# A leaky activation in place of a sign pass, and another order of work, in a fused attention and feed-forward kernel

## The chip, the core and the metric

The kernel runs on one core of one Trainium2 chip. The metric is device time in microseconds (us), from the first to the last instruction with what the runtime puts around them. The core has five engines with queues of their own: TensorE (PE; its weight loads are shown apart as PEld), VectorE (DVE), ScalarE (ACT), GpSimd (POOL) and SyncE (SP), which here only starts DMAs. Each engine works through its queue strictly in order, and waits on semaphores for the others. PE writes to PSUM, and POOL reads and writes SBUF alone.

## The reference

Two parts, one behind the other. The first is a linear attention over 4 batches x 4 heads x 1088 tokens of 32 numbers, in float32; the second a feed-forward layer of width 2048 on the 4352 tokens of 128 numbers that come out. The weights `w_in` and `w_out` come as float64.

```python
def phi(x):                                   # 8 x 8 products per token and head
    a = np.einsum('rd,bhsd->bhsr', S1, x)
    b = np.einsum('rd,bhsd->bhsr', S2, x)
    return np.einsum('bhsi,bhsj->bhsij', a, b).reshape(*x.shape[:-1], r * r)
q_p, k_p = phi(q), phi(k)
kv  = np.einsum('bhsf,bhsd->bhfd', k_p, v)
z   = np.sum(k_p, axis=2)
num = np.einsum('bhsf,bhfd->bhsd', q_p, kv)
den = np.einsum('bhsf,bhf->bhs', q_p, z)[..., None] + 1e-06
x   = (num / den)                             # -> (4352, 128)

h     = x @ w_in
g     = h * np.clip(h + 3.0, 0.0, 6.0) / 6.0
out   = (g @ w_out).astype(np.float32)
```

## The kernel before, in words

*Tokens.* They are cut into nine chunks: 0 to 7 of 512 tokens, 8 of 256. Keys and values come in nine tiles of 128 tokens per batch, loaded as two groups of 4 and 5 tiles (`k0`, `k1` and `v0`, `v1` are batch 0).

*Attention.* For the keys, `mm_kN` multiplies by S1 and S2 on PE, `cp_kN` copies the result to SBUF on ACT, `outer_kN_t` forms the 8 x 8 products (tile `kph`, on POOL or DVE), and `kvt_b_i` adds up keys times values on PE, in PSUM. Chunk 0 is done the long way: `outer_q0` (tile `qph`), transposes `tr`, copies `trcp`, then `nd` (numerators and denominators, tile written by L499), `norm` on DVE (L504 to L507), the transposes `xt` back (L511), and x split into a high and a low part, `xhi` and `xlo`. Between the key sums and `nd` of batch 0 lie `twice` (ACT copies the sums), `fold` and `zmm` (PE), `spread` (DVE) and `halves` (ACT). Chunks 1 to 8 take a shorter way through `proj`, `cp`, `prod`, `invert`, `divide`, `outer`, `turn`, `move` (eight DMAs) and `xmm`.

*Feed-forward.* For each chunk c and each of eight pairs fp of 128-wide blocks of the 2048, one step: `h` and `l` are six matmuls on PE into a PSUM bank (high x by high and low weights, low x by high weights, L627 to L631), `relu` on ACT (L638), `gate` on DVE (L641), `ghi` on ACT (the high part of g, tile `gh`, L644), `glo` on POOL or DVE (the low part, tile `gl`, L647), then `o` (four matmuls) and `p` (two) by w_out on PE (L664). The first two steps of chunk 0 in the order do `h` in halves of 256 tokens. `h` has two PSUM banks, so the `h` of a step waits for the `gate` of two steps before.

*Weights.* They arrive as raw float64 words, in blocks `wi0` to `wi4` of w_in (256, 256, 512, 512 and 512 columns) and `wo0` to `wo3` of w_out (512 each), and are rebuilt as float32 on the chip: `scale` (ACT, L337) takes the upper 32 bits as a float and multiplies by 2^-112, `sign` (DVE, L343) keeps the sign bit in a PSUM bank, `shift` (DVE, L347) shifts the scaled word left by 3 and puts the sign back, `rest` (ACT, L340) scales the lower 32 bits, `word` (POOL, L351) adds the two, `high` (ACT, L354) and `low` (POOL or DVE, L357) split the result in two parts. The same is done once for S1 and S2, at the start (L291 to L296).

*Loads.* SP starts them one by one (L322); with 128 partitions they have, in KB: S 80, `kN` 256 or 320, `vN` 264 or 330, `qN` 256, weight blocks 256 or 512.

*Order.* `ORDER` is a written list of 1089 steps. `Plan.run` goes through it and emits each step on its engine (`:V` after a name picks DVE where a step may go to two engines, letters in lower case pick a PSUM tag) and hands out buffers in that order. The list alone thus sets each queue. `warm` is a matmul on ones whose result is not used.

Of the kernel before, what the change touches and what calls it, by code (L numbers as in the profile page):

```python
# [14 lines left out]
F32 = mybir.dt.float32  # L15
F32R = mybir.dt.float32r
U32 = mybir.dt.uint32
# [5 lines left out]
P = 128  # L23
# [34 lines left out]
SIGN = 0x80000000  # L58
# [44 lines left out]
s_copy low_wi1 scale_wi2 low_wi0 fold_0 zmm trcp_0_0 scale_wo1 halves tr_0_2:o shift_wi2 nd_0_0 sign_wo1:o shift_wo1 word_wi2 trcp_0_2 rest_wo1
high_wi2 keep_0 ld_q1 ld_k3 ld_k2 ld_wi3 ld_v2 ld_k5 ld_v3 nd_0_2:h norm_0_0 ld_wi4 norm_0_2 xt_0_0:h proj_1:a:o xt_0_2 low_wi2:V cp_1_0 cp_1_1
word_wo1 high_wo1 low_wo1 prod_1 xhi_0_0 xhi_0_1 mm_k2 mm_k3 ld_wo0 ld_q3 ld_q2 cp_k2 cp_k3 scale_wi3 xlo_0_0 xlo_0_1 h_0_3_1 l_0_3_1 rest_wi3
outer_k2_0:V sign_wi3:o invert_1 outer_k2_2:V shift_wi3 h_0_0_1_0 h_0_3_0 l_0_3_0 relu_0_3 l_0_0_1_0 h_0_0_0_0 h_0_0_1_1 kvt_1_0:o l_0_0_0_0 h_0_0_0_1
l_0_0_1_1 l_0_0_0_1 kvt_1_1 relu_0_0 outer_k3_2:V gate_0_3 outer_k3_0 outer_k3_4 divide_1 outer_1_1 mm_k5 kvt_1_2 kvt_1_3 kvt_1_4 kvt_1_5 kvt_1_6
kvt_1_7 kvt_1_8 h_0_2_0 h_0_2_1 l_0_2_0 l_0_2_1 word_wi3 outer_1_0 cp_k5 high_wi3 ghi_0_3 twice_1 scale_wi4 ld_k4 gate_0_0 turn_1_1 h_0_1_0_0
l_0_1_0_0 h_0_1_0_1 l_0_1_0_1 fold_1 h_0_1_1_0 turn_1_0 sign_wi4:o relu_0_2 low_wi3 rest_wi4 scale_wo0 keep_1 glo_0_3 l_0_1_1_0 h_0_1_1_1 l_0_1_1_1
o_0_3 outer_k5_4:V shift_wi4 word_wi4 move_1 ld_wo2 ld_q4 ld_v4 p_0_3 ld_v5 ld_wo3 ghi_0_0 gate_0_2 sign_wo0:h shift_wo0 proj_23:o:a ld_k6 ld_q5  # L110
h_0_5_1 h_0_5_0 l_0_5_1 l_0_5_0 relu_0_1 glo_0_0 ghi_0_2 o_0_2 rest_wo0 high_wi4 relu_0_5 outer_k5_0:V cp_2_0 gate_0_1 h_0_4_1 l_0_4_1 h_0_4_0 l_0_4_0
cp_2_1 outer_k5_2:V cp_3_1 cp_3_0 word_wo0 mm_k4 xmm_1:a:o high_wo0 low_wi4 relu_0_4 prod_3 low_wo0 gate_0_5 xhi_1_1 xhi_1_0 h_0_6_0 h_0_6_1 l_0_6_0
l_0_6_1 gate_0_4 h_1_1_0 h_1_1_1 ghi_0_1 o_0_1 relu_0_6 glo_0_2:V xlo_1_0 xlo_1_1 cp_k4 l_1_1_1 l_1_1_0 relu_1_1 ghi_0_4 glo_0_1 invert_3 gate_0_6
p_0_2 outer_k4_0:V o_0_0 h_1_2_0 h_1_2_1 l_1_2_1 l_1_2_0 p_0_0 divide_3 prod_2 outer_3_0 gate_1_1 h_0_7_0 h_0_7_1 invert_2 p_0_1 l_0_7_0 l_0_7_1
glo_0_4:V scale_wo2 relu_1_2 ghi_1_1 relu_0_7 outer_k4_2:V kvt_2_0 kvt_2_1 kvt_2_2 kvt_2_3 kvt_2_4 kvt_2_5 kvt_2_6 kvt_2_7 kvt_2_8 divide_2 outer_3_1
outer_2_0 glo_1_1 gate_1_2 h_1_3_0 h_1_3_1 l_1_3_1 l_1_3_0 rest_wo2 twice_2 o_1_1 fold_2 out_0_3 ghi_1_2 glo_1_2 turn_3_0 turn_3_1 gate_0_7 h_1_0_1
h_1_0_0 l_1_0_0 l_1_0_1 p_1_1 sign_wo2 o_1_2 shift_wo2 sign_wo3:o keep_2 scale_wo3 relu_1_3 relu_1_0 rest_wo3 turn_2_0 shift_wo3 ld_q7 p_1_2
proj_45:a:o gate_1_3 h_1_5_0 ghi_1_3 ghi_0_5 gate_1_0 h_1_7_0 l_1_7_0 h_1_7_1 h_1_5_1 l_1_5_0 ghi_1_0 l_1_5_1 o_1_3 outer_2_1 word_wo2 word_wo3
# [24 lines left out]
o_5_4 p_5_1 p_4_7 xlo_6_0 glo_5_4 relu_5_5 xlo_6_1 h_6_0_1 l_6_0_1 h_6_0_0 l_6_0_0 glo_5_2:V glo_4_6 o_4_6 p_4_4 relu_6_0 ghi_5_0 glo_5_0 gate_5_5
h_6_4_0 o_5_7 p_5_2 o_5_2 l_6_4_0 h_6_4_1 l_6_4_1 relu_6_4 gate_6_0 ghi_6_0 h_5_3_0 l_5_3_0 h_5_3_1 l_5_3_1 o_5_0 p_4_6 ghi_5_5 glo_5_7 xlo_7_1 p_5_7
gate_6_4 h_6_2_0 h_6_2_1 l_6_2_1 l_6_2_0 p_5_0 o_5_5 glo_5_5:V relu_5_3 gate_5_3 h_6_1_0 h_6_1_1 l_6_1_1 l_6_1_0 relu_6_2 ghi_6_4 out_4_7 glo_6_4
# [88 lines left out]
def fused_kernel(ctx: ExitStack, tc: tile.TileContext, inputs, places, outT):  # L234
# [18 lines left out]
    def at(buf):  # L253
        return room[buf.tag][buf.slot]
# [73 lines left out]
    def weights(nm, hi, lo, j):  # L328
# [24 lines left out]
        def high(_):  # L353
            nc.scalar.copy(hi, at(wb)[:, :n])  # L354
# [406 lines left out]
```

## Time and profile before

| | |
|---|---|
| three runs, median | 228.77 us (228.6 to 228.99) |
| the profiled execution | 227.95 us, of which its span is 226.2 us |
| PE busy | 219.7 us, 97% of the span |
| DVE, ACT, POOL busy | 163.1, 165.9 and 153.7 us |
| HBM read and written | 11.30 MB and 2.23 MB |

The span runs from the first to the last instruction; all times below count from its start. "Idle before" of an instruction is how long its engine had done nothing, with what it waited for behind an arrow. The lengths of PE's matmuls overlap: one is shown with its latency, so the pace is the distance from one start to the next.

### The profile page before, as it was taken

To read this page: it belongs to the slowest core of one execution; us is meant where nothing else is said; L and a number is where in the kernel's file an instruction comes from. 1 tells how busy PE (TensorE), PEld (TensorE's weight loads), DVE (VectorE), ACT (ScalarE), POOL (GpSimd) and SP (SyncE) were. 2 spreads that over 40 slices of the span, in tenths; PEclk is the share of its full clock that TensorE was granted. 3 is DMA by queue.
4 is the path that set the end of the run, shared out by engine and by line. 5 is a ranking of instruction groups with operands and counts; after the bars stand their busy time and mean duration, and the time that the engine had idled before them with its cause. 6 is when DMAs were issued, how large, how long until landed. Compare 5 with 4: busy or idle time off the path is not lost.

```text
span 226.2 us, 4762 instructions
## 1 busy us (share of the span) xinstructions
PE 219.7 (97%) x1888; PEld 174.9 (77%) x1888; DVE 163.1 (72%) x216; ACT 165.9 (73%) x231; POOL 153.7 (68%) x111
## 2 busy tenths in 40 slices
PE   8789999999999999999999999999999999999994
PEld 3568768877788788777887888788888788888993
DVE  2799999999949889677866865686378644648561
ACT  4687997989785878656687865876686777785781
POOL 3859998998199734993899797356640498564471
PEclk9999999999999999999999999999999999999999
DMA  6997149233600001233001113020010000020010
GB/s 206 395 412 281 48 118 380 82 83 78 193 3 0 3 0 47 50 81 130 0 1 48 49 46 93 25 71 0 0 46 3 0 0 0 3 93 0 0 51 23
DMA packets 9430, 17.77 MB, mean 79 GB/s; under 512 B 1728, under 2 KB 2368, under 8 KB 9408
## 3 DMA queue, kind: packets, MB, share of 16 engines
q1 hardware_dynamic: 9408, 17.46, 23.2%
q8 instruction: 15, 0.25, 0.5%
q14 instruction: 7, 0.06, 0.1%
HBM read 11.30 MB, written 2.23 MB: 60 GB/s over the span
## 4 chain that ended last, share of the span: by engine, by line
PE 87%; DVE 5%; POOL 3%; DMA 1%; ACT 1%; issue 0%; SPq 0%; DVEq 0%
PE o L664 41%; PE h L627 14%; PE h L631 13%; PE h L628 13%; PE a L547 2%; DMA raw<-weights_dram 1%; DVE kph L385 1%; PE o L405 1%; PE a L542 1%; POOL gl L647 1%; DVE o L343 1%; POOL w L351 1%; DVE w L347 1%; PE a L375 1%; POOL wi_lo L357 1%; POOL kph L385 0%
## 5 line engine op out<-in xcount | busy, mean ns | idle before, releaser
L647 POOL TENSOR_TENSOR gl<-g,gh 128x1024 fp32r<-128x1024 f32 (+1 forms) x45 | 106.3, 2372 | 56.7 <-ACT gh L644 38.4
L641 DVE SCALAR_TENSOR_TENSOR g<-g,h 128x1024 f32<-128x1024 f32 (+1 forms) x72 | 82.8, 1153 | 35.4 <-ACT g L638 35.2
L638 ACT ACTIVATE g<-h 128x1024 f32<-128x1024 f32 (+1 forms) x72 | 70.7, 982 | 35.3 <-PE h L631 20.7
L644 ACT CAST gh<-g 128x1024 fp32r<-128x1024 f32 (+1 forms) x72 | 70.2, 1002 | 11.0 <-DVE g L641 6.0
L627 PE MATMUL h<-xh,wi_hi 128*128 128x512 f32 (+1 forms) x148 | 56.2, 381 | 0.0
L628 PE MATMUL h<-xh,wi_lo 128*128 128x512 f32 (+1 forms) x148 | 55.1, 373 | 0.0
L664 PE MATMUL o<-gh,wo_hi 128*128 128x512 f32 (+1 forms) x144 | 54.2, 379 | 0.0
L664 PE MATMUL o<-gh,wo_lo 128*128 128x512 f32 (+1 forms) x144 | 54.0, 378 | 0.0
L631 PE MATMUL h<-xh,wi_hi 128*128 128x512 f32 (+1 forms) x148 | 49.9, 374 | 0.0
L664 PE MATMUL o<-gl,wo_hi 128*128 128x512 f32 (+1 forms) x144 | 41.3, 380 | 0.1
L647 DVE TENSOR_TENSOR gl<-g,gh 128x1024 fp32r<-128x1024 f32 (+1 forms) x27 | 33.1, 1235 | 5.9 <-PE o L664 3.6
L627 PEld LDWEIGHTS h<-xh,wi_hi 128*128 128x128 f32 x148 | 27.8, 188 | 7.5 <-DVE g L641 1.2
L631 PEld LDWEIGHTS h<-xh,wi_hi 128*128 128x128 f32 x148 | 27.7, 188 | 5.5 <-DVE xh L470 0.2
L628 PEld LDWEIGHTS h<-xh,wi_lo 128*128 128x128 f32 x148 | 27.8, 188 | 4.6
L664 PEld LDWEIGHTS o<-gh,wo_hi 128*128 128x128 f32 x144 | 27.1, 188 | 5.3 <-issue 0.4
L664 PEld LDWEIGHTS o<-gh,wo_lo 128*128 128x128 f32 x144 | 27.1, 188 | 4.9
L664 PEld LDWEIGHTS o<-gl,wo_hi 128*128 128x128 f32 x144 | 26.0, 188 | 5.5 <-POOL gl L647 0.5
L590 POOL TENSOR_TENSOR qph<-ab 128x512 f32<-128x512 f32 (+1 forms) x16 | 16.1, 1018 | 0.2
L351 POOL TENSOR_TENSOR w<-w,r 128x512 int32<-128x512 int32 (+1 forms) x9 | 10.4, 1166 | 2.5 <-DVE w L347 2.0
L597 DVE STREAM_TRANSPOSE raw<-qph 128x512 f32<-128x512 f32 (+1 forms) x16 | 10.4, 665 | 1.9 <-POOL qph L590 1.9
L385 DVE TENSOR_TENSOR kph<-a,ab 128x512 f32<-128x512 f32 (+1 forms) x14 | 8.8, 635 | 0.5 <-ACT ab L378 0.5
L405 PE MATMUL o<-kph,v 128*32 128x64 f32 x288 | 6.2, 223 | 1.1 <-DVE kph L385 1.0
(104 smaller groups left out, 160.1 us busy)
## 6 DMA issues: line engine op xcount, KB each, us to landing
raw<-weights_dram SPq DMA_DIRECT2D x7, 512.0 KB, 6.3
phT<-raw SPq DMA_DIRECT2D x56, 64.0 KB, 2.0
qT<-tokens_dram SPq DMA_DIRECT2D x8, 256.0 KB, 6.0
outT_dram<-os SPq DMA_DIRECT2D x8, 256.0 KB, 2.2
v<-tokens_dram SPq DMA_DIRECT2D x4, 330.0 KB, 4.8
kT<-tokens_dram SPq DMA_DIRECT2D x4, 320.0 KB, 5.7
v<-tokens_dram SPq DMA_DIRECT2D x4, 264.0 KB, 6.1
kT<-tokens_dram SPq DMA_DIRECT2D x4, 256.0 KB, 5.7
```

Source lines behind the costliest of these rows:

```text
L351: nc.gpsimd.tensor_tensor(w, w, at(rb)[:, :n], op=ALU.add)
L385: engines[e].tensor_tensor(out, a_, b_, op=ALU.mult)
L590: engines[e].tensor_tensor(out, a_, b_, op=ALU.mult)
L597: nc.vector.transpose(turned_view()[:, :, r * half : (r + 1) * half].rearrange("p f (t w) -> p t f w", w=Q), src)
L627: nc.tensor.matmul(at(hb)[:, u, i:k], wi_hi[:, f], x, start=True, stop=False)
L628: nc.tensor.matmul(at(hb)[:, u, i:k], wi_lo[:, f], x, start=False, stop=False)
L631: nc.tensor.matmul(at(hb)[:, u, i:k], wi_hi[:, f], at(x_buf[c])[:, 1, i:k], start=False, stop=True)
L638: nc.scalar.activation(at(gb)[:, :, :n], at(hb)[:, :, :n], AF.Relu, bias=3.0, scale=1.0)
L641: nc.vector.scalar_tensor_tensor(at(gb)[:, :, :n], at(gb)[:, :, :n], 6.0, at(hb)[:, :, :n], op0=ALU.min, op1=ALU.mult)
L644: nc.scalar.copy(at(gh)[:, :, :n], at(gb)[:, :, :n])
L647: engines[e].tensor_tensor(at(gl)[:, :, :n], at(gb)[:, :, :n], at(gh)[:, :, :n].bitcast(F32), op=ALU.subtract)
L664: nc.tensor.matmul(at(ob)[:, :n], w, x[:, :n], start=left == acc["all"] and i == 0, stop=left == 1 and i == len(pairs) - 1)
```

## The change

1. `scale` becomes a leaky activation (`Prelu`) with the slope -2^32 for negative inputs. A negative word comes out positive with its exponent raised by 32, and the shift by 3 moves that bit to the sign's place. So `sign` is gone, and `shift` is a shift with one input, in place. The same holds for S1 and S2.
2. `rest`, `word`, `high`, `cp_k`, `trcp`, `xhi` and `ghi` may run on one of two engines, as the order says.
3. `far_queries` may take chunks of different sizes together; the groups of chunks stay (1), (2, 3), (4, 5), (6, 7), (8).
4. `ORDER` is another list, found by a search in which loads came as late as recorded and all durations were varied at random. It has 8 `warm` in place of 11. 19 `ghi`, 7 `xhi`, 2 `rest`, a `cp_k`, a `word` and a `high` now go to DVE, and of `glo` 33 in place of 27, of `low` 3 in place of 2.

```diff
-SIGN = 0x80000000
+SIGN = -(2.0**32)
 ORDER = """
-ld_k0 warm warm warm warm warm warm warm s_rep s_tr mm_k0:h ld_wi0 scale_wi0 warm warm warm s_back ld_k1 mm_k1 sign_wi0:o shift_wi0 rest_wi0 cp_k0 outer_k0_2 ld_wi1 sign_wi1 outer_k0_0:V
+s_copy warm warm warm warm warm warm s_rep ld_k0 ld_k1 warm mm_k0:a cp_k0 outer_k0_0 outer_k0_2:V mm_k1:a cp_k1 outer_k1_2 outer_k1_0:V ld_q0 mm_q0:h
...
+    def copy(e, out, src):
+        (nc.scalar.copy if e == ACT else engines[e].tensor_copy)(out, src)
...
         def scale(_):
-            nc.scalar.activation(at(wb)[:, :n], words(at(raw)[:, :n])[0].bitcast(F32), AF.Copy, bias=0.0, scale=REBIAS)
+            nc.scalar.activation(at(wb)[:, :n], words(at(raw)[:, :n])[0].bitcast(F32), AF.Prelu, bias=0.0, scale=REBIAS, alpha=SIGN)
...
-        def sign(_):
-            nc.vector.tensor_scalar(bank(sb_)[:, :n].bitcast(U32), words(at(raw)[:, :n])[0], SIGN, None, op0=ALU.bitwise_and)
+        def rest(e):
+            low = words(at(raw)[:, :n])[1]
+            if e == ACT:
+                nc.scalar.activation(at(rb)[:, :n], low, AF.Copy, bias=0.0, scale=2.0**-29)
+            else:
+                nc.vector.tensor_scalar(at(rb)[:, :n], low, 2.0**-29, None, op0=ALU.mult)
         def shift(_):
             w = at(wb)[:, :n].bitcast(U32)
-            nc.vector.scalar_tensor_tensor(w, w, 3, bank(sb_)[:, :n].bitcast(U32), op0=ALU.logical_shift_left, op1=ALU.bitwise_or)
+            nc.vector.tensor_scalar(w, w, 3, None, op0=ALU.logical_shift_left)
...
-        b = plan.add(f"rest_{name}", ACT, [ld], rest, [raw, rb])
-        o = plan.add(f"sign_{name}", DVE, [ld], sign, [raw, sb_])
-        o = plan.add(f"shift_{name}", DVE, [a, o], shift, [wb, sb_])
-        o = plan.add(f"word_{name}", POOL, [o, b], word, [wb, rb])
-        o = plan.add(f"high_{name}", ACT, [o], high, [wb])
+        b = plan.add(f"rest_{name}", (ACT, DVE), [ld], rest, [raw, rb])
+        o = plan.add(f"shift_{name}", DVE, [a], shift, [wb])
+        o = plan.add(f"word_{name}", (POOL, DVE), [o, b], word, [wb, rb])
+        o = plan.add(f"high_{name}", (ACT, DVE), [o], high, [wb])
...
-            a = plan.add(f"xhi_{c}_{k}", ACT, after, xhi, [xps, xh])
+            a = plan.add(f"xhi_{c}_{k}", (ACT, DVE), after, xhi, [xps, xh])
...
-        high = plan.add(f"ghi_{c}_{fp}", ACT, [o], ghi, [gb, gh])
+        high = plan.add(f"ghi_{c}_{fp}", (ACT, DVE), [o], ghi, [gb, gh])
```

The loads on SP, from the start of the program, before (`raw` is a weight block: here `wi0`, `wi1`, `wi2`, `wo1`; `kT` holds keys, `qT` queries, `v` values):

```order
L288 DMA sb_raw<-weights_dram 128x80
L322 DMA kT_78<-tokens_dram 128x512
L322 DMA raw_74<-weights_dram 128x256
L322 DMA kT_79<-tokens_dram 128x640
L322 DMA raw_75<-weights_dram 128x256
L322 DMA qT_81<-tokens_dram 128x512
L322 DMA v_127<-tokens_dram 128x528
L322 DMA v_128<-tokens_dram 128x660
L322 DMA raw_76<-weights_dram 128x512
L322 DMA raw_77<-weights_dram 128x512
L322 DMA qT_82<-tokens_dram 128x512
L322 DMA kT_80<-tokens_dram 128x640
```

and now (`raw` is `wi1`, `wi0`, `wi2`, `wo1`):

```order
L291 DMA sb_raw<-weights_dram 128x80
L324 DMA kT_78<-tokens_dram 128x512
L324 DMA kT_79<-tokens_dram 128x640
L324 DMA qT_81<-tokens_dram 128x512
L324 DMA v_127<-tokens_dram 128x528
L324 DMA raw_74<-weights_dram 128x256
L324 DMA v_128<-tokens_dram 128x660
L324 DMA raw_75<-weights_dram 128x256
L324 DMA raw_76<-weights_dram 128x512
L324 DMA qT_82<-tokens_dram 128x512
L324 DMA raw_77<-weights_dram 128x512
L324 DMA kT_80<-tokens_dram 128x512
L324 DMA kT_78<-tokens_dram 128x640
```

Keys, queries and values of batch 0 move ahead of the first blocks of w_in, and `wi0` goes from third to eighth place.

DVE's queue from S's words on, before (`w` is a weight block, `o` and `a` PSUM banks with sign bits, `kph` and `qph` outer products):

```order
L294 SCALAR_TENSOR_TENSOR s_word<-s_word,s_sign 128x80
L343 TENSOR_SCALAR o_70<-raw_74 128x256
L347 SCALAR_TENSOR_TENSOR w_119<-w_119,o_70 128x256
L343 TENSOR_SCALAR a_72<-raw_75 128x256
L385 TENSOR_TENSOR kph_88<-h_68,ab_84 128x512
L347 SCALAR_TENSOR_TENSOR w_120<-w_120,a_72 128x256
L385 TENSOR_TENSOR kph_89<-a_73,ab_85 128x512 x2
L385 TENSOR_TENSOR qph_90<-h_69,ab_86 128x512 x2
L343 TENSOR_SCALAR o_71<-raw_76 128x512
L427 TENSOR_TENSOR z_diag<-mask,o_70 128x256
```

and now (L346 is `rest`, L360 `low`):

```order
L296 TENSOR_SCALAR s_word<-s_word 128x80
L387 TENSOR_TENSOR kph_88<-a_72,ab_84 128x512
L387 TENSOR_TENSOR kph_89<-a_73,ab_85 128x512
L387 TENSOR_TENSOR qph_90<-h_68,ab_86 128x512
L350 TENSOR_SCALAR w_119<-w_119 128x256
L387 TENSOR_TENSOR qph_90<-h_68,ab_86 128x512
L346 TENSOR_SCALAR r_122<-raw_75 128x256
L350 TENSOR_SCALAR w_120<-w_120 128x256
L360 TENSOR_TENSOR wi_lo<-w_119,wi_hi 128x256
L429 TENSOR_TENSOR z_diag<-mask,o_70 128x256
```

The outer products come first, and of the three of keys that DVE had one goes to POOL; the sign passes are gone, and `spread` (`z_diag`) comes as the tenth row in both.

PE's queue around the first feed-forward matmul, before (`h1` takes chunk 0's x back from the transpose by `ident`, `s_all` is S, `kT` the keys of batch 1):

```order
L511 MATMUL h1_69<-ident_132,x0_94 128x128 x2
L542 MATMUL a1_73<-qT1_82,s_proj_146 32x256 x4
L542 MATMUL o1_71<-qT1_82,s_proj_146 32x256 x4
L511 MATMUL h1_69<-ident_132,x0_94 128x128 x2
L375 MATMUL a0_72<-s_all_162,kT0_78 32x2x32 x16
L375 MATMUL a1_73<-s_all_162,kT2_80 32x2x32 x20
L627 MATMUL h0_68<-xh0_95,wi_hi_64 128x512
```

and now:

```order
L546 MATMUL a0_72<-qT1_82,s_proj_146 32x256 x4
L546 MATMUL o0_70<-qT1_82,s_proj_146 32x256 x4
L513 MATMUL h1_69<-ident_132,x0_94 128x128 x2
L377 MATMUL a1_73<-s_all_160,kT2_80 32x2x32 x16
L513 MATMUL h1_69<-ident_132,x0_94 128x128 x2
L377 MATMUL a0_72<-s_all_160,kT0_78 32x2x32 x20
L632 MATMUL h0_68<-xh0_95,wi_hi_64 128x256
```

The first group of batch 1's keys now stands between the two transposes, and the first feed-forward step works on half of the chunk.

## Rows read from the trace of the kernel before

**Rows 1.** The page: busy time, and slices of PE and its granted clock.

```profile
PE 219.7 (97%) x1888; PEld 174.9 (77%) x1888; DVE 163.1 (72%) x216; ACT 165.9 (73%) x231; POOL 153.7 (68%) x111
...
PE   8789999999999999999999999999999999999994
...
PEclk9999999999999999999999999999999999999999
```

**Rows 2.** The chain that ended last, in order of time: start, length, what.

```profile
78.91 2.27 PE o L664 x10
...
218.60 4.33 PE o L664 x36
```

**Rows 3.** Timeline of PE: start, length, instruction [idle before <- releaser].

```profile
9.92 0.32 PE L405 MATMUL o<-kph,v 128*32 128x64 f32 x8 [1.04 <-DVE kph L385]
...
10.75 0.66 PE L489 MATMUL a<-ident,qph 128*128 128x128 f32 x4
...
13.22 0.69 PE L499 MATMUL a<-kvb,phT 128*64 128x66 f32 x16
...
15.89 0.44 PE L511 MATMUL h<-ident,x 128*128 128x128 f32 x2
16.26 1.21 PE L375 MATMUL a<-s_all,kT 128*32 128x64 f32 x72
17.41 0.50 PE L627 MATMUL h<-xh,wi_hi 128*128 128x512 f32 x1
...
26.77 0.40 PE L664 MATMUL o<-gh,wo_lo 128*128 128x512 f32 x1
27.25 0.73 PE L664 MATMUL o<-gl,wo_hi 128*128 128x512 f32 x2
```

**Rows 4.** Timeline of DVE: S's words, signs and shifts, the norms.

```profile
2.64 0.20 DVE L293 TENSOR_SCALAR s_sign<-sb_raw 128x80 uint32<-128x80 uint32 x1 [0.93 <-DMA sb_raw<-weights_dram]
2.95 0.24 DVE L294 SCALAR_TENSOR_TENSOR s_word<-s_word,s_sign 128x80 uint32<-128x80 uint32 x1
...
6.74 0.43 DVE L343 TENSOR_SCALAR a<-raw 128x256 uint32<-128x256 uint32 x1 [1.03 <-DMA raw<-weights_dram]
...
13.41 0.69 DVE L347 SCALAR_TENSOR_TENSOR w<-w,o 128x512 uint32<-128x512 uint32 x1
14.02 0.16 DVE L504 TENSOR_SCALAR den<-a 128x8 f32<-128x8 f32 x1
...
14.79 0.16 DVE L504 TENSOR_SCALAR den<-h 128x8 f32<-128x8 f32 x1
```

**Rows 5.** Timeline of ACT: passes that waited for a weight block.

```profile
4.75 0.45 ACT L337 ACTIVATE w<-raw 128x256 f32<-128x256 f32 x1 [1.68 <-DMA raw<-weights_dram]
...
10.19 0.70 ACT L340 ACTIVATE r<-raw 128x512 int32<-128x512 uint32 x1 [0.58 <-DMA raw<-weights_dram]
```

**Rows 6.** Windows: stretch, PE, PEld, DVE, ACT, POOL busy, clock, DMA, GB/s.

```profile
40.00:50.00 10.00, 10.00 (x136) 7.95 (x135) 9.93 (x15) 8.63 (x16) 9.46 (x8) 1.00 0.23 65
60.00:80.00 20.00, 20.00 (x176) 15.96 (x154) 14.99 (x20) 14.96 (x19) 15.51 (x11) 1.00 0.07 25
```

**Rows 7.** Timeline of DVE: two subtractions of a low part.

```profile
56.48 1.86 DVE L647 TENSOR_TENSOR gl<-g,gh 128x1024 fp32r<-128x1024 f32 x1
...
147.60 1.22 DVE L647 TENSOR_TENSOR gl<-g,gh 128x1024 fp32r<-128x1024 f32 x1
```

**Rows 8.** Timeline of POOL: instructions beside those of rows 7 and rows 4.

```profile
12.66 1.28 POOL L351 TENSOR_TENSOR w<-w,r 128x512 int32<-128x512 int32 x1 [1.62 <-DVE w L347]
...
55.97 1.30 POOL L357 TENSOR_TENSOR wo_lo<-w,wo_hi 128x512 fp32r<-128x512 f32 x1
...
148.26 2.83 POOL L647 TENSOR_TENSOR gl<-g,gh 128x1024 fp32r<-128x1024 f32 x1 [5.05 <-PE o L664]
```

**Rows 9.** The key loads started in the first 30 us.

```profile
DMA to landing us min/median/max: 2.6/6.7/8.4
```

**Rows 10.** Groups of DVE by line and shape: busy us, mean ns.

```profile
L647 DVE TENSOR_TENSOR gl<-g,gh 128x1024 fp32r<-128x1024 f32 x24 | 30.9, 1294 | 4.8 <-PE o L664 2.5 <-ACT gh L644 1.9 <-ACT ab L378 0.4
```

More of the change, by code (lines that the diff above doesn't have):

```diff
@@ L103 @@
[L103 to L106, printed above, removed]
@@ L333, in weights, with word, high @@
         ld, raw = load("raw", name, lambda t: t[:, :n])
-        wb, rb, sb_ = Buf(("w",)), Buf(("r",)), Buf(ANY)
+        wb, rb = Buf(("w",)), Buf(("r",))
         def scale(_):
-            nc.scalar.activation(at(wb)[:, :n], words(at(raw)[:, :n])[0].bitcast(F32), AF.Copy, bias=0.0, scale=REBIAS)
-        def rest(_):
-            nc.scalar.activation(at(rb)[:, :n], words(at(raw)[:, :n])[1], AF.Copy, bias=0.0, scale=2.0**-29)
-        def sign(_):
-            nc.vector.tensor_scalar(bank(sb_)[:, :n].bitcast(U32), words(at(raw)[:, :n])[0], SIGN, None, op0=ALU.bitwise_and)
+            nc.scalar.activation(at(wb)[:, :n], words(at(raw)[:, :n])[0].bitcast(F32), AF.Prelu, bias=0.0, scale=REBIAS, alpha=SIGN)
[5 more added lines that the diff above has]
+                nc.vector.tensor_scalar(at(rb)[:, :n], low, 2.0**-29, None, op0=ALU.mult)
         def shift(_):
             w = at(wb)[:, :n].bitcast(U32)
-            nc.vector.scalar_tensor_tensor(w, w, 3, bank(sb_)[:, :n].bitcast(U32), op0=ALU.logical_shift_left, op1=ALU.bitwise_or)
-        def word(_):
+            nc.vector.tensor_scalar(w, w, 3, None, op0=ALU.logical_shift_left)
+        def word(e):
             w = at(wb)[:, :n].bitcast(I32)
-            nc.gpsimd.tensor_tensor(w, w, at(rb)[:, :n], op=ALU.add)
-        def high(_):
-            nc.scalar.copy(hi, at(wb)[:, :n])
+            engines[e].tensor_tensor(w, w, at(rb)[:, :n], op=ALU.add)
+        def high(e):
+            copy(e, hi, at(wb)[:, :n])
         def low(e):
@@ L387, in features @@
         o1 = plan.add(f"mm_{name}", PE, [ld], mm, [src, pb, ab])
-        o2 = plan.add(f"cp_{name}", ACT, [o1], cp, [pb, ab])
+        o2 = plan.add(f"cp_{name}", (ACT, DVE), [o1], cp, [pb, ab])
         parts = []
@@ L513, in queries @@
             a = plan.add(f"tr_{c}_{t}", PE, [parts[t], parts[t + m - 1]], tr, [ph, pb, phT])
-            a = plan.add(f"trcp_{c}_{t}", ACT, [a], trcp, [pb, phT])
+            a = plan.add(f"trcp_{c}_{t}", (ACT, DVE), [a], trcp, [pb, phT])
             a = plan.add(f"nd_{c}_{t}", PE, [a, kv_done["near"]], nd, [phT, nb, x])
@@ L520, in far_queries @@
     def far_queries(cs):
-        n = CHUNKS[cs[0]][1]
-        half, blocks = n // 2, n // 2 // Q
+        sizes = [CHUNKS[c][1] for c in cs]
+        offs = [sum(sizes[:k]) // 2 for k in range(len(cs))]
         pbs, xpbs = ([Buf(("a", "o")) for _ in range(2)] for _ in range(2))
@@ L526, in far_queries @@
         for k, c in enumerate(cs):
-            c0 = CHUNKS[c][0]
+            c0, n = CHUNKS[c]
+            half = n // 2
             cuts = [i for i in range(n) if i in (0, half) or batch_of(c0 + i) != batch_of(c0 + i - 1)] + [n]
             spans += [(k, i // half, batch_of(c0 + i), i, j) for i, j in zip(cuts, cuts[1:])]
-            lq, qb = load("qT", f"q{c}", lambda t: t[:, :n])
+            lq, qb = load("qT", f"q{c}", lambda t, n=n: t[:, :n])
             loads.append(lq)
@@ L536, in part @@
         def part(banked, k, r, i, j):
-            return bank(banked[r])[:, k * half + i - r * half : k * half + j - r * half]
+            i0 = offs[k] - r * sizes[k] // 2
+            return bank(banked[r])[:, i0 + i : i0 + j]
         def proj(_):
@@ L550, in far_queries @@
         for k, c in enumerate(cs):
-            moves.append(quotient(c, n, projected_by, [(pbs[r], k * half) for r in range(2)], moved[k]))
+            moves.append(quotient(c, sizes[k], projected_by, [(pbs[r], offs[k]) for r in range(2)], moved[k]))
         xhs = [Buf(("xh",)) for _ in cs]
@@ L554, in far_queries @@
         for k, c in enumerate(cs):
-            split(c, [(k * half, r * half, (r + 1) * half, [o], xpbs[r]) for r in range(2)], xhs[k])
+            half = sizes[k] // 2
+            split(c, [(offs[k], r * half, (r + 1) * half, [o], xpbs[r]) for r in range(2)], xhs[k])
     def quotient(c, n, o, sources, phT):
@@ L641, in gate, with ghi @@
             nc.vector.scalar_tensor_tensor(at(gb)[:, :, :n], at(gb)[:, :, :n], 6.0, at(hb)[:, :, :n], op0=ALU.min, op1=ALU.mult)
-        def ghi(_):
-            nc.scalar.copy(at(gh)[:, :, :n], at(gb)[:, :, :n])
+        def ghi(e):
+            copy(e, at(gh)[:, :, :n], at(gb)[:, :, :n])
         def glo(e):
```

133 lines of the change are left out of this document (68 added, 65 removed).

## The prediction

> **What bounds the kernel now.** Read the page's busy line and slices first [rows 1]: PE is busy 97% of the span, at 7 or 8 tenths in the first three slices of 40 and 9 in every later one but the last, and the granted clock reads 9 throughout. The chain that ended last says the same [rows 2]: stretches of PE alone, ten 512-column matmuls in 2.27 us (0.227 each) at 79 us, and 36 of 256 columns in 4.33 us (0.120 each) up to 222.93. So a matmul in the middle is neither late nor slow. Only less work on PE, or an earlier start of the pile, can shorten the run, and the work is the same in both kernels. The feed-forward part has 756 matmuls of 512 columns (8 chunks x 8 pairs x 12, less the 12 that chunk 0 does in halves) and 120 of 256 (those 24 halves, and chunk 8's 96): 171.6 + 14.4 = 186.0 us. Its first one starts at 17.41 [rows 3], and from there to 222.93 are 205.5 us; the 19.5 left over are attention work of the later batches and chunks, with a small loss at each switch between the two kinds. PE's timeline shows one clear wait behind 17.41: a matmul starts at 26.77, the next could at 27.00, and it starts at 27.25 [rows 3].
>
> What is left to look at is the 17.41 us in front. There PE waits for others, 1.04 us for key features from DVE at 9.92 [rows 3], then for copies, norms and transposes that follow each other. DVE is the engine that is full early on: 9.93 of 10 us from 40 to 50, against 14.99 of 20 from 60 to 80 [rows 6].
>
> **The change, part by part.**
>
> *Sign pass gone.* Ten DVE instructions vanish: 0.20 us on the S words, 0.43 for each of the two 256-wide blocks, and for each of seven 512-wide ones 0.69 (I take the shift's row of that width): 5.9 us. Four of the blocks' passes (2.2 us) stand ahead of the first norm [rows 4].
>
> *The shift alone.* It had two inputs, one in PSUM, and took 0.69 at 512 wide [rows 4]. Now it has one and stays in SBUF. The nearest rows are the two on the S words, both 80 wide and SBUF to SBUF: 0.20 with one input, 0.24 with two [rows 4]. From 256 to 512 wide a pass grows by 0.26 (0.43 to 0.69), 0.0010 per element, so 0.04 is 40 of the 80 elements: the one-input form runs at half the time per element, 0.42 at 512 wide. Bounds 0.42 and 0.69; I take 0.42, since that row has the form itself. DVE saves another 2 us by it.
>
> *Leaky activation for a scaled copy.* No row shows one. Bounds: the copy's time (0.45 at 256 wide, 0.70 at 512 [rows 5]) or twice that. I take the copy's, the same instruction with another function. Twice would put 0.45 + 0.70 + 0.70 more on ACT ahead of the second norm, some 1.4 us with the waits it has there, and that is the whole gain below.
>
> *Work that may go to DVE.* 19 of 72 `gh` copies, 7 of 18 x copies, two `rest` passes, six more `gl` subtractions (33 for 27) and a few of the weights' last steps go there. A subtraction with two SBUF inputs takes 1.22 [rows 7]; a copy as wide lies between that and, at half the time per element, 0.68. With 0.68 the copies are 13 us, the subtractions 7, the rest some 5, and DVE goes from 163 to about 180 of 226. The first `gh` copy that moves is in chunk 1, past 60 us, where DVE has 5 of 20 us free [rows 6]; that room hides them. Without it each would hold the next gate, and PE, which eats a pair in 2.7 us (12 x 0.227).
>
> *Loads in another order.* SP starts them in turn, and the bytes come at one rate: block 0 of w_in is there at 4.75, block 2 at 10.19 [rows 5], with 1938 KB from the one to the other, 356 KB per us. By that rate the new order brings k0 at 4.0, k1 at 4.9, q0 at 5.7, v1 at 8.0 (8.8 before) and block 0 of w_in at 8.75.
>
> *The path to the first matmul.* Before: the last five key tiles' sums run from 9.92 to 10.75, the numerators start at 13.22, the two norms at 14.02 and 14.79, the last transpose at 15.89, batch 1's keys take 16.26 to 17.41 [rows 3, 4]. After:
> - Key sums: the outer products stand first on DVE, with no weight pass between, so v1 decides: start 8.1, and with the same 0.83 the end is at 8.95.
> - ACT copies the sums. Ahead of that copy stand two weight passes, the first of which waits for w_in's block 0: 8.75 + 0.45 + 0.45 = 9.65. Before, the copy could start as the sums ended, at 10.75. This point is 1.1 us earlier.
> - From there to the numerators it took 13.22 - 10.75 = 2.47. ACT now has a 256-wide cast (I take 0.45) where a 512-wide pass (0.70) was: 2.2. Numerators at 11.9.
> - First norm 0.8 later (14.02 - 13.22), at 12.7. The second came 0.77 behind it; a 512-wide shift (0.42) now stands between: 13.9.
> - Last transpose 1.10 later (15.89 - 14.79), at 15.0, and 0.37 long (to 16.26). Of batch 1's keys 16 of 36 matmuls now stand ahead of it; the other 20 take 20/36 of 1.15, 0.64. First matmul at 16.0.
>
> That is 1.4 us earlier. Behind it, up to some 43 us, DVE loses three sign passes and gains on three shifts (3 x 0.96 = 2.9), and takes over an x copy and a subtraction (0.4 + 1.2): 1.3 less, about what PE starts earlier. So PE should wait no more than before; I count neither the 0.25 at 27.25 as won nor a new wait as lost.
>
> **A rule weighed.** A DVE subtraction with two SBUF inputs that starts at 56.48, with POOL in an instruction until 57.27, takes 1.86 in place of 1.22 [rows 7, 8]; a POOL one that starts at 148.26, with DVE in such a subtraction until 148.82, takes 2.83 [rows 7, 8]. They wait for each other's end. The old shift did not: at 13.41 it takes its 0.69 beside a POOL add that runs until 13.94 [rows 4, 8]. The Trainium skill ("SBUF — State Buffer", section "SBUF: two separate sides") says that DVE and GpSimd share a port pair which one of them holds for a whole instruction, and that DVE takes it with two SBUF inputs and in a two-port performance mode too. The rows agree on the first; none shows the second. If it holds, the new shifts and copies join the subtractions in waiting for POOL, and that is the last rival below, priced from rows.
>
> **Sum.** The profiled execution took 227.95 around its span of 226.2; 227.95 - 1.4 = 226.55. The runs' median is 228.77, 0.8 above; 228.77 - 1.4 = 227.4. What differs by under 0.2% (0.46 us) can't be told from no change.
>
> **Rivals.**
> - *More.* ACT's copy of the sums comes right behind them at 9.2 (w_in's block 0 early by as much), and the 0.25 goes too: 1.4 + 0.45 + 0.25 = 2.1, 226.7; with the shift between the norms hidden as well (0.42), 226.2. For it: fewer DVE passes everywhere. Against: block 0 stands behind v1 in the queue. Chance 0.17.
> - *Nothing.* Batch 1's keys now stand on PE around the last transpose, so their load is in front of everything. By the rate k3 (3874 KB in) is there at 14.0, against a need at 15.4; of the key loads before one took 8.4 us from issue to landing [rows 9]. If it lands at 16.8, or the leaky activation takes twice the copy, the gain is gone: 228.8. Chance 0.13.
> - *Slower.* The ports: three shifts and two or three subtractions on DVE lie between the first matmul and 43 us, where POOL has hardly a pause (9.46 of 10 us from 40 on [rows 6]). At 0.64 each (1.86 - 1.22) they add 3.2 to 3.8 us to DVE, against the 1.3 it has less to do and the 1.4 won: 0.5 to 1.1 slower, 229.6. It decides from 2.7 us of such waits on. For it: the rows on waits, and DVE full to 9.93 of 10. Against: the 24 full subtractions of this trace take 1.294 on average [rows 10], so most met no wait. Chance 0.13.
>
> **Chances.** Forecast (0.9 to 1.9 less) 0.57, *more* 0.17, *nothing* 0.13, *slower* 0.13. So faster 0.74, within 0.2% 0.13, slower 0.13. The range takes in all of *nothing*, most of *more* and the nearer part of *slower*, 226.0 to 229.0.
>
> **What will show it.** The first feed-forward matmul between 15.5 and 16.5, the last key sums from about 8.1, the numerators at 11.9; shifts of 0.42 and leaky activations of 0.70 at 512 wide; from the first matmul to the end of PE 205.5 or a little less. Wrong would be: a first matmul at 17 or later; PE idle behind DVE's gates between 20 and 45; shifts of 1 us and more that end as a POOL instruction ends; a slice of the granted clock below 9.

## The result, and the profile after

The changed kernel takes 226.12 us (median of 4 runs, 225.89 to 226.47), the kernel before 228.82 beside it (228.6 to 228.99): a ratio of 0.9883, 95% interval 0.9867 to 0.9899, or 2.7 us. The forecast was 227.4, 1.4 us less than before. The sign was right, the size half of what came.

The page of the changed kernel: busy time of PE and DVE, two rows of the 40 slices, the chain's shares.

```profile
PE 218.4 (97%) x1885; PEld 175.5 (78%) x1885; DVE 182.2 (81%) x244; ACT 147.7 (66%) x201; POOL 144.2 (64%) x103
...
PE   8889999999999999999999999999999999999994
...
PEclk9999999999999999999999999999999999999998
...
PE 93%; DMA 2%; SPq 1%; ACT 1%; issue 1%
```

PE is the bound as before, with an 8 where [rows 1] has a 7; DVE went from 163 to 182 us, as forecast (about 180). The timeline of PE ahead of the first feed-forward matmul (start, duration, work, idle time in brackets) answers to [rows 3]:

```profile
8.74 0.32 PE L407 MATMUL o<-kph,v 128*32 128x64 f32 x8 [0.67 <-DMA v<-tokens_dram]
...
12.06 0.69 PE L501 MATMUL o<-kvb,phT 128*64 128x66 f32 x16 [0.56 <-ACT kvb L438]
...
13.88 0.33 PE L513 MATMUL h<-ident,x 128*128 128x128 f32 x1
14.71 0.27 PE L513 MATMUL h<-ident,x 128*128 128x128 f32 x1 [0.50 <-issue]
14.91 0.65 PE L377 MATMUL a<-s_all,kT 128*32 128x64 f32 x32
15.49 0.44 PE L513 MATMUL h<-ident,x 128*128 128x128 f32 x2
15.86 0.77 PE L377 MATMUL a<-s_all,kT 128*32 128x64 f32 x40
16.56 0.39 PE L632 MATMUL h<-xh,wi_hi 128*128 128x256 f32 x1
```

The last five key tiles start when v1 is there (8.74 for 9.92), the numerators at 12.06 for 13.22, the first feed-forward matmul at 16.56 for 17.41. ACT's and DVE's timelines, against [rows 4] and [rows 5]: copy of the sums, leaky activation of 512 columns, norm, shift of 512, norm.

```profile
9.96 0.26 ACT L441 COPY kvt<-o 128x128 f32<-128x128 f32 x1
...
10.72 0.68 ACT L339 ACTIVATE w<-raw 128x512 f32<-128x512 f32 x1
```

```profile
12.80 0.17 DVE L506 TENSOR_SCALAR den<-o 128x8 f32<-128x8 f32 x1 [0.60 <-PE o L501]
...
13.57 0.42 DVE L350 TENSOR_SCALAR w<-w 128x512 uint32<-128x512 uint32 x1
13.91 0.16 DVE L506 TENSOR_SCALAR den<-h 128x8 f32<-128x8 f32 x1
```

Two more traces, one of each kernel, were taken later. Side by side, worked out from the starts of all matmuls (a matmul's share is the time to the next start; "lost at switches" is what the row ahead of work of another kind and the row behind it take beyond 0.227 or 0.120, the first feed-forward matmul among them):

| us | before | before again | after | after again |
|---|---|---|---|---|
| profiled execution | 227.95 | 229.31 | 226.31 | 226.14 |
| last part of k1 lands | 5.52 | 7.51 | 4.86 | 4.91 |
| first feed-forward matmul | 17.41 | 18.80 | 16.56 | 16.78 |
| from there to PE's end | 205.51 | 205.48 | 204.62 | 204.36 |
| of it: switches, lost at them | 17, 3.28 | 17, 3.27 | 11, 2.23 | 11, 2.22 |
| of it: other losses of feed-forward rows | 0.75 | 0.53 | 0.45 | 0.45 |
| of it: attention work, its waits within | 15.31 | 15.50 | 15.77 | 15.51 |

The rest, 186.17 us in each, is the feed-forward work that the prediction counted as 186.0. So about 1.0 us (0.86 to 1.15) came behind the first feed-forward matmul, where none was forecast, by these rows mostly from six switches fewer. And the trace that the sum started from was of an execution whose loads came early: of 73 runs of before, in five comparisons, one was below its 227.95.

### The profile page after: what moved, and what is told of

Same layout as the page of the kernel before. It is cut to its first block, busy times and chain, and to the rows that moved or that the text cites. A ratio compares the mean times of both kernels' runs of the same rounds, so it can differ in the third digit from the quotient of the medians.

```text
span 224.4 us, 4722 instructions
## 1 busy us (share of the span) xinstructions
PE 218.4 (97%) x1885; PEld 175.5 (78%) x1885; DVE 182.2 (81%) x244; ACT 147.7 (66%) x201; POOL 144.2 (64%) x103
## 3 DMA queue, kind: packets, MB, share of 16 engines
HBM read 11.30 MB, written 2.23 MB: 60 GB/s over the span
## 4 chain that ended last, share of the span: by engine, by line
PE 93%; DMA 2%; SPq 1%; ACT 1%; issue 1%
PE o L669 42%; PE h L632 14%; PE h L633 14%; PE h L636 14%; DMA raw<-weights_dram 2%; PE o L407 2%; PE a L377 2%; PE a L546 1%; PE a L551 1%; SPq L324 1%; PE o L551 1%; ACT w L339 1%; PE o L546 0%; PE h L513 0%; PE o L501 0%
## 5 line engine op out<-in xcount | busy, mean ns | idle before, releaser
L652 POOL TENSOR_TENSOR gl<-g,gh 128x1024 fp32r<-128x1024 f32 (+1 forms) x39 | 92.1, 2364 | 60.9 <-ACT gh L254 34.2
L254 ACT CAST gh<-g 128x1024 fp32r<-128x1024 f32 (+1 forms) x53 | 53.2, 1011 | 19.3 <-PE o L669 16.7
L632 PE MATMUL h<-xh,wi_hi 128*128 128x512 f32 (+1 forms) x148 | 55.8, 378 | 0.0
L636 PE MATMUL h<-xh,wi_hi 128*128 128x512 f32 (+1 forms) x148 | 52.7, 372 | 0.0
L652 DVE TENSOR_TENSOR gl<-g,gh 128x1024 fp32r<-128x1024 f32 (+1 forms) x33 | 40.8, 1238 | 4.6 <-ACT gh L254 3.6
L254 DVE CAST gh<-g 128x1024 fp32r<-128x1024 f32 (+1 forms) x19 | 14.9, 785 | 3.5 <-PE o L669 3.3
L354 POOL TENSOR_TENSOR w<-w,r 128x512 int32<-128x512 int32 (+1 forms) x8 | 9.8, 1230 | 3.9 <-DVE w L350 2.4
L387 DVE TENSOR_TENSOR kph<-a,ab 128x512 f32<-128x512 f32 (+1 forms) x15 | 9.3, 642 | 2.3 <-ACT ab L254 2.2
```

What stands on the lines that cost most here:

```text
L254: (nc.scalar.copy if e == ACT else engines[e].tensor_copy)(out, src)
L354: engines[e].tensor_tensor(w, w, at(rb)[:, :n], op=ALU.add)
L387: engines[e].tensor_tensor(out, a_, b_, op=ALU.mult)
L632: nc.tensor.matmul(at(hb)[:, u, i:k], wi_hi[:, f], x, start=True, stop=False)
L636: nc.tensor.matmul(at(hb)[:, u, i:k], wi_hi[:, f], at(x_buf[c])[:, 1, i:k], start=False, stop=True)
L652: engines[e].tensor_tensor(at(gl)[:, :, :n], at(gb)[:, :, :n], at(gh)[:, :, :n].bitcast(F32), op=ALU.subtract)
```

## The experiments

Ratios are against runs of before on the same chip; the changed kernel's was 0.9883 and 0.9902.

**Both kernels again.** The same code, for second traces.

> The changed kernel once more, beside the edits of it below, and with a second trace. All theories: 0.98 to 0.99 of before. If the start of the first feed-forward matmul belongs to the order, it is again at 16.5 to 16.7; if the landing of the first loads differs from one execution to the next (in the first trace of after it was 16.56, in that of the kernel with the cut stretch, whose first 30 us stand in the same order, 17.29), it will be at another place, by up to 0.7 us.

> The kernel before once more, for a second trace. Its profiled execution took 227.95 where the median of its runs is 228.6 to 228.8; two traces of after end their matmuls at 221.18 and 221.14. If the first trace was of a quick execution, this one ends later than 222.92 and shows at which place: by the landing of the first loads (first feed-forward matmul later than 17.41) or by waits behind it. Rival (the two traces of after are the quick ones): this one is within 0.2 us of the first.

After: 226.33, 0.9902 (0.9878 to 0.9926), first feed-forward matmul at 16.78. Before: 229.31 in the one execution. PE's timeline of before again:

```profile
5.05 0.83 PE L281 MATMUL o<-const-bfloat16-1.0 128*128 128x512 bf16 x3
7.55 1.23 PE L375 MATMUL a<-s_all,kT 128*64 128x64 f32 x18 [1.68 <-DMA kT<-tokens_dram]
...
18.80 0.50 PE L627 MATMUL h<-xh,wi_hi 128*128 128x512 f32 x1
```

PE waits 1.68 us for k1 at 7.55, and the end is later by the same 1.4 as the first feed-forward matmul (224.28 and 222.92). A load lands in sixteen parts, and in each trace single parts fall about 1 us or more behind the rest at some moment, and stay behind in the loads after it. In four traces with the old order of loads, where k1 stands behind block 0 of w_in, it was whole at 5.52, 6.35, 7.18 and 7.51; in ten with the new one, where it comes next to k0, at 4.84 to 5.40. Later in the queue a part falls behind in all 14, in seven of the ten at k2 or k3, which are needed only at 15. There it lands 0.9 to 1.5 us behind the rest of a load that comes in while the first 16 KB packet of the instruction queue is under way, or just behind it (before: packet 11.67 to 12.60, k3 whole at 14.02, its other parts at 12.79; after: packet 12.33 to 13.26, k3 at 14.76 and 13.87). All 14 agree in this, but no run moved the packet on purpose, and beside the early delays of k1 there is none: why those come is not shown.

**The operations alone.** The order of before without its nine sign words:

```
- o = plan.add(f"sign_{name}", DVE, [ld], sign, [raw, sb_])
- o = plan.add(f"shift_{name}", DVE, [a, o], shift, [wb, sb_])
+ o = plan.add(f"shift_{name}", DVE, [a], shift, [wb])
```

> The order of before with the operations of after: the ten sign passes are left out, the scaled copy is the leaky activation, the shift has one input. The trace of after against that of before (221.18 and 222.92 at PE's end, 1.74 apart) gives two candidates. Path theory (the prediction's): fewer DVE passes ahead of the key features and the norms bring the first feed-forward matmul forward; here PE waits 1.04 us at 9.92 for key features behind two sign passes and a shift on DVE, so 0.5 to 0.9 us faster than before. Switch theory: what the new order saves lies behind the first feed-forward matmul, where PE leaves the feed-forward matmuls for another kind 11 times in after and 17 in before, each time losing 0.09 us at the last matmul before and 0.11 at the first behind (3.17 and 2.13 us in sum); this kernel keeps the 17, so that none of this 1.0 us comes. Rival (the order alone did it): within 0.2 us of before.

229.15 us, 1.0022 (1.0007 to 1.0038): no gain, rather 0.5 lost, and the path theory's 0.5 to 0.9 did not come. The first feed-forward matmul is at 17.77, and from there to the end are 206.08, 0.6 more than before; no single wait accounts for it. DVE's first passes go, but they stood where DVE waited for loads or for ACT's copies anyway. DVE's, POOL's and PE's timeline show what is new:

```profile
13.23 1.02 DVE L342 TENSOR_SCALAR w<-w 128x512 uint32<-128x512 uint32 x1 [0.62 <-ACT w L335]
14.30 0.17 DVE L498 TENSOR_SCALAR den<-a 128x8 f32<-128x8 f32 x1
```

```profile
12.70 1.27 POOL L346 TENSOR_TENSOR w<-w,r 128x512 int32<-128x512 int32 x1 [1.68 <-DVE w L342]
```

```profile
13.57 0.69 PE L493 MATMUL a<-kvb,phT 128*64 128x66 f32 x16 [0.37 <-ACT kvb L430]
```

The one-input shift takes 1.02 in place of 0.43, since a POOL add runs until 13.97; the old one took its 0.69 beside such an add [rows 4, 8]. The norm comes at 14.30, 0.28 later than before, but not by the shift: the numerators that it needs start 0.35 later (13.57 for 13.22), in a trace where block 2 of w_in lands at 10.59 for 10.10, and in after the norm follows them by 0.74. The Trainium skill ("SBUF — State Buffer", section "SBUF: two separate sides") has it that a DVE instruction in a two-port mode and a GpSimd one shut each other out of a shared pair of ports, whichever starts first; the row agrees with the waiting, and shows nothing of the mode.

**The order alone.** After, with the sign passes and two-input shifts back (`sign_wi1:a shift_wi1`, and so on ahead of each shift):

> The order of after with the operations of before: a sign pass into a PSUM bank directly ahead of each shift, the shift with two inputs, the scaled copy without the leaky activation. If the passes on DVE are what the path is made of (the prediction's step), the three blocks ahead of the norms cost 0.43 + 0.14 twice and 0.69 + 0.27 once, of which 1.0 us or more shows at the end: 1.0 to 1.6 us slower than after. Switch theory: the 11 switches stay, so at least 1.0 us of the gain over before is kept: 0.3 to 1.0 us slower than after. Rival (the order alone): within 0.2 us of after.

232.69 us, 1.018 (1.0155 to 1.0205): 6.5 slower than after, worse than any theory had it. It keeps the 11 switches (2.24 lost), but the first feed-forward matmul is at 17.71, and PE's list of waits (us in total, times, longest) has DVE in it:

```profile
PE h L638 <- DVE g L652: 3.0, 3, 1.4
PE a L383 <- DVE w L355: 1.0, 1, 1.0
...
PE h L638 <- DVE w L355: 0.6, 1, 0.6
```

L355 is the two-input shift, L652 the gate behind such passes. So neither half of the change wins anything by itself: the new order has no room for the old passes.

**The copies back on ACT.** First all 30, then the 19 of `gh` alone (`ghi_1_7:V` becomes `ghi_1_7`):

> After, with the 30 copies that its order gives to DVE back on ACT (19 of gh, 7 of x, one of the features, one of a weight block, two rest passes), all else in its place. The prediction said that room on DVE hides these copies and counted them at nothing. If moving them was worth nothing, this is within 0.3 us of after; if it was what took waits away behind the first feed-forward matmul, it is 0.5 us or more slower. The two rest passes stand ahead of the norms and put 0.4 + 0.7 us on ACT there: up to 0.5 us of a loss may be theirs, which the trace will tell by the start of the first feed-forward matmul (16.56 in after).

> After, with only the 19 copies of gh that DVE has got back on ACT, in their places. With 30 copies back it was 9.0 us slower, of which the trace showed 1.9 ahead of the first feed-forward matmul (18.44 for 16.56) and most of the rest in a few waits of PE behind it (2.34 us at 79.1, with eight matmuls behind it at half the pace, 0.8 at 123.4, 0.58 at 209.7). Theory (the gates' low part needs the high part early, and ACT with its relus is late with it): first feed-forward matmul at 16.5 to 17.3 as in after, the waits behind it stay, 4 to 7 us slower than after. Rival (the loss came from the passes in front and a shifted order behind them): within 1 us of after.

235.12 us, 1.0271 (1.0235 to 1.0306), and 231.49, 1.0142 (1.011 to 1.0175). With all 30 the first feed-forward matmul is late too, at 18.43. With the 19 alone the first feed-forward matmul stays (16.82) and the loss is behind it, as the theory said. Around 76 us of that kernel, in PE's, ACT's and POOL's timeline, and POOL's same subtraction in after:

```profile
76.01 0.40 PE L636 MATMUL h<-xh,wi_hi 128*128 128x512 f32 x1
78.58 0.73 PE L669 MATMUL o<-gl,wo_hi 128*128 128x512 f32 x2 [2.17 <-POOL gl L652]
```

```profile
75.06 1.04 ACT L254 CAST gh<-g 128x1024 fp32r<-128x1024 f32 x1
```

```profile
76.17 2.35 POOL L652 TENSOR_TENSOR gl<-g,gh 128x1024 fp32r<-128x1024 f32 x1 [4.25 <-ACT gh L254]
```

```profile
73.62 2.42 POOL L652 TENSOR_TENSOR gl<-g,gh 128x1024 fp32r<-128x1024 f32 x1 [1.76 <-DVE gh L254]
```

ACT ends the copy at 76.1 behind a relu, POOL's subtraction starts only then and takes 2.35, and PE waits for it; in after, with the copy on DVE, it starts at 73.62. The copies are hidden on DVE as forecast, and this order depends on them. It isn't shown that another order could not do without.

**What a switch costs.** One stretch of attention work cut into seven (`kvt_2_4` behind `l_1_2_1`, `kvt_2_5` behind `p_0_1`, ...), then, in before, two joined:

> After, with the one stretch at 35.8 us in which PE does the nine key tiles of batch 2 and 32 key-feature matmuls cut into seven, feed-forward work between them: the same instructions, and their operands are there before. Switch theory: six more switches at 0.09 + 0.11 = 0.20 us, 1.2 us slower than after. Rival (the losses at a switch belong to late operands, not to the switch): within 0.3 us of after.

> The kernel before, with one of its 17 switches taken out: the first key tile of batch 1, which stands alone between feed-forward matmuls at 19.83 (10 matmuls in 0.29 us, 0.09 lost at the row before, 0.10 at the row behind), moved to the other eight at 20.90, where ten take 0.145. Switch theory: the stretch from the first feed-forward matmul to the end, 205.5 in both traces of before, is 0.34 us shorter, 205.1 to 205.2, and the loss at the rows around switches 3.07 for 3.27; in the runs 0.1 to 0.2% faster, which five rounds may just tell. Rival (the loss at a switch is hidden by waits that PE has anyway in this stretch): 205.5, no change.

The cut: 229.17, 1.0022 (1.0004 to 1.004), 3 us slower than after. Two cuts in PE's timeline:

```profile
40.34 0.40 PE L636 MATMUL h<-xh,wi_hi 128*128 128x512 f32 x1
40.66 0.32 PE L407 MATMUL o<-kph,v 128*32 128x64 f32 x8
40.80 0.22 PE L410 MATMUL o<-ab 128*32 128x32 f32 x2
40.95 0.73 PE L669 MATMUL o<-gl,wo_hi 128*128 128x512 f32 x2
41.61 0.32 PE L407 MATMUL o<-kph,v 128*32 128x64 f32 x8
```

From 40.34 to 40.66 are 0.32 where a matmul takes 0.227, and from 40.95 to 41.61 two take 0.66 for 0.454: 0.2 a switch, as expected (3.49 lost at 17 switches, 2.22 at 11). Besides, ten matmuls alone take 0.29 us, 0.145 each ten in a longer stretch. So a switch more costs about 0.35, six 2.1; the rest is a wait of 0.93 for a gate and later loads in front (first feed-forward matmul at 17.29).

The join: 228.96, 0.9997 (0.9976 to 1.0018), no change. 16 switches lose 3.08, 0.19 less, as expected, but from the first feed-forward matmul to the end are 205.49, as in both traces of before. PE's timeline has a wait in the stretch that took the tile in:

```profile
22.55 0.59 PE L375 MATMUL a<-s_all,kT 128*32 128x64 f32 x27 [0.17 <-issue]
```

The rival's result came, but its reason, a wait that PE had there anyway, isn't what the row shows: "issue" is a wait for nothing that the profile sees, like the stops in the last section (a packet of the instruction queue had ended at 21.21, 1.34 us before). And the runs, with 0.2% either way, can't tell the 0.34 that was expected from nothing. That a switch more costs is shown; that one less wins is not.

**The path in front.** The copy of the sums, mask product and folding ahead of the weight passes (its edit, in short, stands below); that, with v1 loaded ahead of block 1 of w_in and the key features of k3 behind the first feed-forward matmuls; the first again, with the norms ahead of those passes too:

```
- scale_wi0 word_wi1 high_wi1 warm kvt_0_3 ... kvt_0_8 twice_0 rest_wi0:V tr_0_0:o trcp_0_0 ... spread
+ word_wi1 warm kvt_0_3 ... kvt_0_8 twice_0 spread scale_wi0 high_wi1 rest_wi0:V tr_0_0:o trcp_0_0 fold_0 zmm
```

> After, with the copy of the key sums, the product with the mask and the folding put ahead of the weight passes that stand before them on ACT, DVE and PE. The prediction's path: the sums end at 9.5 and are copied at 9.96, behind two weight passes of which the first waits for block 0 of w_in; the numerators start at 12.06. If that path sets the end, the copy moves to 9.5, the numerators to 11.3 to 11.6, and the end comes 0.4 to 0.7 us earlier than after. Rival (the weights' passes, which go back by as much, or the loads of batch 1's keys set the first feed-forward matmul): within 0.2 us of after or slower.

> After, with the first 17 us in another order: v1 is loaded ahead of block 1 of w_in, the steps from the key sums to the numerators stand ahead of the weight passes, and the last 20 key tiles' matmuls of batch 1 behind the first feed-forward pair (one switch more). Path theory: PE loses the 0.67 us that it waits for v1 and most of the 0.56 us for the copied sums, 0.35 come back for the switch: 0.6 to 1.2 us faster than after. Rival (the order behind the first feed-forward matmul is cut to the moments of after, and gives the time back in waits for weights or gates): within 0.3 us of after or slower.

> The kernel with the sums' copy and the folding first was no faster than after (0.9919 and 0.9902 of before), and its trace shows why: the numerators started at 11.82 for 12.3 in the trace of after beside it, but the first norm stood behind two weight passes on DVE (13.20 for 13.0) and the second numerators behind two on ACT (0.93 us). Here both norms also stand ahead of those passes, and the copy for the second numerators ahead of them on ACT. Path theory: first norm at 12.5, first feed-forward matmul at 15.8 to 16.4 (16.6 and 16.8 in after), 0.3 to 0.8 us faster than after. Rival (the load of the next keys, 14.5 and 15.2 in the trace, or the weights' passes that now come later hold PE): within 0.2 us of after, or slower by waits of PE between 18 and 25 us.

226.91, 0.9919 (0.9897 to 0.9942); 228.73, 1.0 (0.9978 to 1.0023); 227.9, 0.9948 (0.993 to 0.9967): none is faster than after. In the first the numerators come at 11.82, but DVE's timeline has the norm behind a shift that waited for ACT:

```profile
12.52 0.43 DVE L350 TENSOR_SCALAR w<-w 128x512 uint32<-128x512 uint32 x1 [0.28 <-ACT w L339]
12.86 0.42 DVE L360 TENSOR_TENSOR wi_lo<-w,wi_hi 128x256 fp32r<-128x256 f32 x1
13.20 0.16 DVE L506 TENSOR_SCALAR den<-o 128x8 f32<-128x8 f32 x1
```

In the last the norm is at 12.49, but ACT's copy of the first transposes comes at 15.45, behind a weight pass that waits until 14.88 for its buffer (one of two, which a DVE subtraction holds until 14.79), and PE idles; the busy time by stretches (PE, PEld, DVE, ACT, POOL with counts, then the granted clock) shows what that costs:

```profile
13.00:16.00 3.00, 1.43 (x23) 0.53 (x20) 2.15 (x7) 1.58 (x6) 1.39 (x1) 1.00 1.03 403
16.00:19.50 3.50, 3.50 (x78) 2.95 (x78) 3.23 (x9) 2.74 (x6) 2.99 (x4) 0.52 0.39 122
```

After 3.00 us with PE busy 1.43 the granted clock is 0.52, close to the lower of its two levels (1.2 of 2.4 GHz), and 72 key-feature matmuls take 2.31 us for 1.21 [rows 3]. The second kernel has it too, 0.52 from 18 to 21. The path theory as I put it falls: one step earlier only meets the next engine's order.

**More work in front.**

```
+ for t in list(range(n)) * (2 if name == "k3" else 1):
```

> After, with the 40 matmuls of the key features of block 3, the last work ahead of the first feed-forward matmul, done twice over: 0.64 us more on PE there, nothing else changed. The prediction's sum takes each microsecond in front of the first feed-forward matmul as one at the end: then 0.6 us slower than after, and the stretch from that matmul to the end as long as in after (204.4 to 204.6). Rival (part of it is given back behind, where PE waited for gates and loads): 0 to 0.3 us slower, and the stretch shorter by as much.

231.73, 1.0134 (1.0096 to 1.0172), 5.5 slower than after for 0.64 us of work, and so no answer to its question. The first feed-forward matmul stays at 16.74, since the stop of 0.50 that after has at 14.71 does not come here, and PE stops elsewhere, with a granted clock of 0.68 from 24.2 to 28.5.

```profile
21.33 0.61 PE L377 MATMUL a<-s_all,kT 128*32 128x64 f32 x30
24.18 0.35 PE L377 MATMUL a<-s_all,kT 128*32 128x64 f32 x9 [2.24 <-issue]
```

That a microsecond in front is one at the end is shown by the two traces of before instead (1.39 later, 1.36 later).

## Why the prediction came out as it did

- **What bounds.** Right: PE alone, 186.17 us of feed-forward work in every trace.
- **Loads.** Right in order, and in size but for v1, block 0 of w_in and k3: 8.60, 9.30 and 14.76 for 8.0, 8.75 and 14.0. "The bytes come at one rate" is what failed: parts fall behind by about 1 us or more at a moment that differs, and with the old order k1 was late by it in three of four traces. The forecast of 1.4 in front was made against a trace in which it was not. By the median run, 228.8, PE's end would be at 223.8 (5.03 less in both traces of before), and 205.5 ahead of it 18.3: 1.5 to 1.7 in front against 16.56 and 16.78, an estimate. That this is near the 1.4 is in part luck: against the trace that the sum started from, 0.85 and 0.63 came. No run put the new order of loads into the kernel before, so what it is worth alone is not shown.
- **The path.** Right step by step, none over 0.65 late: sums from 8.74 (8.1), copy 9.96 (9.65), numerators 12.06 (11.9), norms 12.80 and 13.91 (12.7 and 13.9), last transpose 15.49 (15.0), first feed-forward matmul 16.56 (16.0). What v1 was late is down to 0.16 at the numerators; the rest comes with the stop of 0.50 at 14.71. Counted from the landing of v1, the first feed-forward matmul comes 8.57, 8.51, 8.47 and 8.53 us later in the four traces with the old order of loads (before, before again, the operations alone, the join), 7.96 and 7.93 in the two of after, where the prediction had 8.6 and 8.0. So the path is shorter by 0.6 with the stop in it, and the rest in front is v1 itself: 8.60 and 8.85 in after, 8.84, 10.29, 9.30 and 10.15 in those four.
- **Operations.** Shift 0.42, leaky activation 0.68 (taken as 0.42 and 0.70): right. But the saving of DVE passes alone is not what won: without the new order it gives nothing.
- **Behind the first feed-forward matmul.** The step that failed is the term of zero there, "neither the 0.25 at 27.25 as won nor a new wait as lost". The text named "a small loss at each switch" and didn't count the switches: 17 before, 11 after, 1.05 us. The 0.25 at 27.25 is in no trace of after, but not in the second of before either, so it belongs to the execution. The attention work takes 0.01 to 0.46 more than before and gives that much back.
- **Rivals.** *More* was nearest in size (226.2 to 226.7), but for another reason: ACT's copy came at 9.96, not 9.2. *Nothing*: the leaky activation costs what the copy did, k3 was there at 14.76. *Slower*: the ports do collide (the shift of 1.02), but in after PE is nowhere idle for over 0.06 us behind the stop at 14.71.

## What to carry to other kernels

Count the switches between kinds of matmul in both orders as well as the work; where PE is the bound, each one more cost about 0.35 us here, and whether one less wins depends on what else PE waits for. Take a second trace before working from one by tenths of a microsecond, and put first what the first engine needs, since a load that is late delays all behind it. A fixed order and its operations are one thing: undoing either half tells that they need each other, not which of them pays.

## What the runs showed of the hardware

- A stop of PE at a fixed place in its program. The 0.50 "issue" at 14.71 comes behind 449 instruction records of PE, and behind 448 or 449 in five other traces (0.47, 0.53, 0.71, 0.48, and 0.23 in the kernel with v1 loaded earlier). With 80 records more in front PE stopped for 2.24 behind 961, 512 further on. In all but the 0.23 a packet of the instruction queue (16 KB) had ended 1.3 to 1.5 us before: 13.26 and 14.71, 13.45 and 14.94, 13.66 and 14.97, 14.01 and 15.44, 13.31 and 14.74, 22.89 and 24.18. The Trainium skill ("Runtime: NRT & Kernel Launch", section "Instruction fetch mechanics") says that instructions come in blocks of 256 and that crossing to the next is mostly hidden; the distance agrees, the hiding doesn't here. Of the ten traces with the new order of work, the five with the stops of 0.47 to 0.71 have the first such packet end latest, at 13.26 to 14.01; in the other five it ended at 11.37 to 13.09, and PE stopped for 0.23 at most. No experiment moved the stop on purpose, and that the fetch is its cause is not shown.
- A switch of PE between feed-forward matmuls and others costs 0.09 at the last row and 0.11 at the first behind; the ten matmuls of a key tile take 0.29 alone, 0.145 more than in a longer stretch.
- An idle PE costs twice: 1.6 us of idling in 3.00 were followed by 3.5 us at a granted clock of 0.52, close to the lower level.
